# The ab times wo3 product of four token groups in Strassen's seven block products

## The chip, the cores and the metric

One core of one Trainium2 chip runs the whole kernel. The metric is the device time of one execution in microseconds (us), lower is better. TensorE does the matmuls, VectorE, ScalarE and GpSimd the work on tiles, and SyncE (SP) issues the DMAs.

## The reference

Attention with 32 packed rows per head gives x of 4608 tokens by 512 columns; a gated layer and a second layer follow. The part that the change touches is the second layer:

```python
x = np.ascontiguousarray(attn_out.transpose(0, 2, 1, 3)).reshape(B * S, H * D)
x = _moe_ref(x=x, **moe_kwargs)              # silu(x@w_gate) * (x@w_val) @ w_out, d_ff 1536
# _moe2_ref: d_model 512, d_ff 1024
a = x @ w1
b = x @ w2
h = a * b @ w3
return (h @ w_out).astype(np.float32)
```

## The kernel before

w3 @ w_out is made once, in float32, as `wo3` (1024 by 512) while the gated layer runs, and lies in the DRAM tile `wo3d`. The last part of the kernel then takes the 4608 tokens in six groups of 768, g = 0 to 5 in the code and 1 to 6 in the text. Each group has two stages.

*Stage 5* makes ab, a times b, transposed, in eight steps f (0 to 7) of 128 columns each. a and b come out of seven block products by Strassen's scheme (`PROD`: bank, sum of x blocks, sum of weight blocks). A product is six matmuls of 128x128 by 128x384 (L1012): each operand is split into a high and a low float32r part, and three of the four cross terms are taken. ScalarE copies four of the products out of PSUM (`keep`, L1027), VectorE and GpSimd add the others to them (`comb`, L1032) and multiply (L1059, L1060). `split` casts the high part on ScalarE (L96) and subtracts it for the low part (L89) on VectorE or GpSimd. The split of a step's ab into `abh` and `abl`, 128x768, is done in the next step, behind its second product.

*Stage 7* multiplies ab by wo3, which lies split in SBUF (`wo_hi`, `wo_lo`), for six tiles of 128 tokens: eight steps f by three terms of 128x128 by 128x512 (L1076). ScalarE copies each tile out (L1078), and SP stores it.

Around this, `x2_prep` loads the next group's x in three, then one DMA of 384 KB (`x2_load`, L831), makes sums of blocks on VectorE (L836) and splits seven of them. The weights' block sums `ws` are made in group 1, each stored to `wsd`, and loaded again in groups 2 to 6, one DMA of 256 KB a product, two steps ahead (`ahead`, L826); step 0's stay in SBUF. In the gated layer `w3_task` fits the work on w3 into free slots; `pin` keeps some of its conversions from being moved earlier by the scheduler.

The engines run their instructions in the order of the program here (`manual_schedule` for the engines in `M0`), and SP issues its DMAs in order too: a DMA that waits holds up those behind it.

Of the kernel before, what the change touches and what calls it, by code (L numbers as in the profile page):

```python
# [8 lines left out]
F32 = mybir.dt.float32  # L9
# [4 lines left out]
ALU = mybir.AluOpType  # L14
# [24 lines left out]
def packed_attention_moe_kernel(  # L39
# [777 lines left out]
    def ws_block(f, k):  # L817

        t = ws_tile(0, f, k)
        split(t[:, 0], t[:, 1], wsrc[f][PROD[k][1]], sub_on="pool" if k % 2 else "dve")  # L820
        if f:
            nc.sync.dma_start(wsd[f, k], t.bitcast(F32).rearrange("p h (d n) -> p h d n", d=2))

    def ws_load(g, f, k):
        t = ws_tile(g, f, k)
        nc.sync.dma_start(t.bitcast(F32).rearrange("p h (d n) -> p h d n", d=2), wsd[f, k])  # L826

    def x2_load(g, i, j):
        t = xp.tile([128, 2, TH], F32, tag="x2r", name=f"x2r{g}_{i}{j}", bufs=3)
# [169 lines left out]
    def split_wo3(r):  # L999
        split(wo3_hi[:, r], wo3_lo[:, r], wo3_t.pop(r))  # L1000

    def stage5(g, f):
        bk = {n: bank(f"p{n}{g}_{f}")[:, 0:TH] for n in "ABC"}
        A, Bk, Cb = (bk[n] for n in "ABC")

        def product(k, first):
            n, _, name = PROD[k]
            xh, xl = x2_t[g, name]
            w = ws_t[f, k]
            for d in range(2):  # L1010
# [128 lines left out]
```

## Time and profile before

| | |
|---|---|
| median of 3 runs | 1357.03 us (1355.51 to 1357.6) |
| profiled execution, its own time | 1358.21 us |
| its span in the profile | 1356.4 us |
| TensorE busy | 1333.3 us, 98% |
| VectorE, ScalarE, GpSimd busy | 48%, 42%, 28% |
| moved by DMA | 230.27 MB, 170 GB/s over the span |
| granted TensorE clock | full in every slice |

Busy time is the sum of what an engine's instructions last, overlaps counted once. A TensorE that is busy for 98% leaves little to wait for, but its matmuls overlap in the pipeline, so the time from the start of one to the start of the next tells more than its duration.

### The profile page before, as it was taken

To read this page: it belongs to the slowest core of one execution; us is meant where nothing else is said; L and a number is where in the kernel's file an instruction comes from. 1 tells how busy PE (TensorE), PEld (TensorE's weight loads), DVE (VectorE), ACT (ScalarE), POOL (GpSimd) and SP (SyncE) were. 2 spreads that over 40 slices of the span, in tenths; PEclk is the share of its full clock that TensorE was granted. 3 is DMA by queue.
4 is the path that set the end of the run, shared out by engine and by line. 5 is a ranking of instruction groups with operands and counts; after the bars stand their busy time and mean duration, and the time that the engine had idled before them with its cause. 6 is when DMAs were issued, how large, how long until landed. Compare 5 with 4: busy or idle time off the path is not lost.

```text
span 1356.4 us, 25516 instructions
## 1 busy us (share of the span) xinstructions
PE 1333.3 (98%) x10196; PEld 1237.9 (91%) x10196; DVE 655.0 (48%) x962; ACT 569.1 (42%) x940; POOL 386.4 (28%) x309
## 2 busy tenths in 40 slices
PE   7889999999999999999999999999999999999998
PEld 5679899999999999999999999899899899998997
DVE  4766877336564466453454389623323334234230
ACT  5774644344443444345544247433333333333331
POOL 1333322323322233244444236312012021121120
PEclk9999999999999999999999999999999999999999
DMA  9977766534545444244453259737458276284441
GB/s 307 345 237 213 220 194 188 167 86 116 153 132 182 122 112 125 71 163 122 129 162 109 74 179 340 277 104 254 147 155 254 81 220 208 94 253 158 143 145 47
DMA packets 186822, 230.27 MB, mean 170 GB/s; under 512 B 70736, under 2 KB 117840, under 8 KB 186704
## 3 DMA queue, kind: packets, MB, share of 16 engines
q1 hardware_dynamic: 186704, 228.64, 53.8%
q8 instruction: 81, 1.33, 0.4%
q14 instruction: 37, 0.30, 0.1%
HBM read 179.04 MB, written 49.55 MB: 169 GB/s over the span
## 4 chain that ended last, share of the span: by engine, by line
PE 81%; DVE 4%; DMA 1%; issue 1%; ACT 1%; SPq 0%; DVEq 0%; ACTq 0%
PE px L674 20%; PE po L1076 14%; PE pA L1012 13%; PE pg L445 10%; PE pv L445 9%; PE pB L1012 6%; PE pw L766 3%; PE pC L1012 3%; PE pc L412 2%; DVE ws L89 1%; PE psq L209 1%; DMA wo3r<-wo3d 0%; DMA x2r<-X2d 0%; DVE x2T L836 0%; DMA X2d<-acc 0%
## 5 line engine op out<-in xcount | busy, mean ns | idle before, releaser
L89 POOL TENSOR_TENSOR ul<-u,uh 128x576 fp32r<-128x576 f32 x96 | 145.7, 1519 | 303.4 <-ACT uh L96 281.5
L1032 POOL TENSOR_TENSOR c<-s,s 128x384 f32<-128x384 f32 x48 | 49.2, 1024 | 376.8 <-ACT s L1027 376.6
L674 PE MATMUL px<-uh,woh 128*128 128x384 f32 x576 | 147.7, 337 | 0.2
L674 PE MATMUL px<-ul,woh 128*128 128x384 f32 x576 | 146.3, 334 | 0.0
L674 PE MATMUL px<-uh,wol 128*128 128x384 f32 x576 | 146.3, 334 | 0.0
L1027 ACT COPY s<-pA 128x384 f32<-128x384 f32 x144 | 69.0, 479 | 179.8 <-PE pA L1012 172.0
L454 DVE TENSOR_TENSOR u<-u,pv 128x576 f32<-128x576 f32 x96 | 71.9, 749 | 134.9 <-PE pv L445 121.1
L1076 PE MATMUL po<-wo_hi,abh 128*128 128x512 f32 x288 | 112.2, 389 | 0.4 <-ACT abh L96 0.4
L1076 PE MATMUL po<-wo_hi,abl 128*128 128x512 f32 x288 | 112.3, 390 | 0.3 <-DVE abl L89 0.3
L1076 PE MATMUL po<-wo_lo,abh 128*128 128x512 f32 x288 | 112.2, 389 | 0.0
L686 DVE TENSOR_TENSOR acc<-acc,px 128x768 f32<-128x768 f32 x72 | 68.1, 950 | 85.1 <-PE px L674 84.6
L674 PEld LDWEIGHTS px<-uh,woh 128*128 128x128 f32 x576 | 102.5, 188 | 6.0 <-issue 3.3
L96 ACT CAST uh<-u 128x576 fp32r<-128x576 f32 x96 | 64.6, 674 | 103.1 <-DVE u L454 102.7
L674 PEld LDWEIGHTS px<-uh,wol 128*128 128x128 f32 x576 | 104.1, 188 | 0.0
L674 PEld LDWEIGHTS px<-ul,woh 128*128 128x128 f32 x576 | 104.0, 188 | 0.0
L450 ACT ACTIVATE u<-pg 128x576 f32<-128x576 f32 x96 | 62.4, 650 | 96.5 <-PE pg L445 90.7
L89 POOL TENSOR_TENSOR wol<-wof,woh 128x512 fp32r<-128x512 f32 x48 | 65.2, 1368 | 127.3 <-ACT woh L96 124.6
L89 DVE TENSOR_TENSOR abl<-ab,abh 128x768 fp32r<-128x768 f32 x48 | 48.1, 1002 | 105.1 <-ACT abh L96 105.0
L445 PE MATMUL pg<-aTh,ch 128*128 128x288 f32 x384 | 83.9, 300 | 1.2 <-DVE cl L89 0.8
L445 PE MATMUL pv<-aTh,ch 128*128 128x288 f32 x384 | 82.9, 297 | 0.9 <-DVE cl L89 0.6
L445 PE MATMUL pg<-aTh,cl 128*128 128x288 f32 x384 | 82.3, 296 | 0.5 <-DVE cl L89 0.5
L445 PE MATMUL pg<-aTl,ch 128*128 128x288 f32 x384 | 82.4, 296 | 0.0
(308 smaller groups left out, 3082.6 us busy)
## 6 DMA issues: line engine op xcount, KB each, us to landing
ws<-wsd SPq DMA_DIRECT2D x245, 256.0 KB, 3.0
wf<-Wd SPq DMA_DIRECT2D x36, 512.0 KB, 5.7
wsd<-ws SPq DMA_DIRECT2D x49, 256.0 KB, 3.2
km<-in_k_dram SPq DMA_DIRECT2D x16, 576.0 KB, 7.6
wof<-wod SPq DMA_DIRECT2D x36, 256.0 KB, 3.0
x2r<-X2d SPq DMA_DIRECT2D x24, 384.0 KB, 5.3
out_dram<-o SPq DMA_DIRECT2D x36, 256.0 KB, 2.0
vm<-in_v_dram SPq DMA_DIRECT2D x16, 512.0 KB, 8.9
```

The lines of the kernel that those rows point to most:

```text
L89: x = eng.tensor_tensor(out=out, in0=src, in1=hi.bitcast(F32), op=ALU.subtract)
L96: nc.scalar.copy(hi, src)
L445: nc.tensor.matmul(t[:, hf, 0:HS], lhsT=w[:, b % 2, Q, cols], rhs=x[:, Q, hf, :], start=first, stop=last,)
L450: x = nc.scalar.activation(u, t[:, :, 0:HS], AF.Silu)
L454: x = nc.vector.tensor_tensor(out=u, in0=u, in1=t[:, :, 0:HS], op=ALU.mult)
L674: nc.tensor.matmul(t[:, h, 0:CW], lhsT=w[:, 128 * d:128 * d + 128], rhs=x[:, CW * c:CW * c + CW], start=first, stop=last,)
L686: pin_at["acc"] = nc.vector.tensor_tensor(out=o, in0=o, in1=t[:, :, 0:CW], op=ALU.add)
L766: nc.tensor.matmul(t[:, 1], lhsT=a[:, kk], rhs=w, start=(i == 0), stop=(i == 11))
L1012: nc.tensor.matmul(bk[n], lhsT=w[:, hl, 128 * d:128 * d + 128], rhs=r[:, d], start=(first and d == 0 and i == 0), stop=(d == 1 and i == 2) ...
L1027: nc.scalar.copy(o, t)
L1032: on.tensor_tensor(out=r, in0=o, in1=t, op=op)
L1076: nc.tensor.matmul(t, lhsT=a[:, j, cols], rhs=w[:, f], start=first, stop=last)
```

## The change

From group 3 on (`GS` = 2 in the code's count) stage 7 becomes `stage7s`: ab in 2x2 blocks of tokens and columns, wo3 in 2x2 blocks, and seven products by the same `PROD`. Each is 3 tiles of tokens x 4 pairs of steps x 3 terms of 128x128 by 128x256. The products add up in PSUM banks A and B, three each, and in four SBUF tiles kA to kD. Stage 5 of these groups splits sums of ab's blocks (`pair_tasks`: A11, S1 to S4, A12, A22, each 128x384) one behind each product of the next step.

wo3's seven sums of blocks are made in group 2 (`wob_task`: four pairs i of rows, each with two loads, four subtracts, seven splits and seven stores to `wobd`), in eight half tiles of the weights' pool. They are loaded again for each product, 1 MB each, three products ahead; for group 3 the first three are loaded during its stage 5. The ws weights are laid out in pairs and, from group 3 on, loaded two products a time, 512 KB, into five buffers, step 0's too. x2's loads stand ahead of the new stage's loads of sums, and its other work behind the products 0, 1 and 2. In `w3_task` the pin no longer covers the conversions; by the scheduler's order four of them (w3_0_0 to w3_0_3, each an activation and a cast on ScalarE) then stand some steps earlier in the gated layer.

```diff
-    wsd = tc.dram_tile([NF2, 7, 128, 2, 2, 128], F32, name="wsd")
+    wsd = tc.dram_tile([NF2 * 7 // 2, 128, 2, 2, 256], F32, name="wsd")
+    wobd = tc.dram_tile([7, 128, NF2 // 2, 2, 256], F32, name="wobd")
...
+            if NH <= i < 2 * NH:
+                pin.update(dve=w3_at[1], act=w3_at[2])
             new = tuple(int(x) for x in w3_list[i - 1].split("_")[1:])
+            pin.clear()
...
-            if NH <= i < 2 * NH:
-                pin.update(dve=w3_at[1], act=w3_at[2])
             w3_conv(w3_list[i])
-            pin.clear()
...
+    GS = 2
+    NPB = NF2 // 2
+    pair_t, wob_t, abT, later = {}, {}, {}, []
+    def ws_pair(n):
+        if n >= (NG2 - GS) * 28:
+            return
+        at, tag = (wgv, ("wh", "wl")[n % 5 % 2]) if n % 5 < 4 else (mp2, "wsx")
+        t = at.tile([128, 2, 2, 256], F32R, tag=tag, name=f"wsp{n}")
+        nc.sync.dma_start(t.bitcast(F32).rearrange("p a h n -> p (a h n)"),
+                          wsd[n % 28].rearrange("p a h n -> p (a h n)"))
+        pair_t[n] = t
...
+    def wob_load(n):
+        if n >= (NG2 - GS) * 7:
+            return
+        if n % 3 == 0:
+            t = [vl.tile([128, 2, 256], F32R, tag=("vt", "vu")[i % 2], name=f"wob{n}_{i}") for i in range(NPB)]
+            for i in range(NPB):
+                nc.sync.dma_start(t[i].bitcast(F32), wobd[n % 7][:, i])
+        else:
+            x = mp2.tile([128, NPB, 2, 256], F32R, tag="wob", name=f"wob{n}", bufs=2)
+            nc.sync.dma_start(x.bitcast(F32).rearrange("p i h n -> p (i h n)"),
+                              wobd[n % 7].rearrange("p i h n -> p (i h n)"))
+            t = [x[:, i] for i in range(NPB)]
+        wob_t[n] = t
...
+    def wob_task(i, n):
+        if n == 0:
+            e, o = (vl.tile([128, DM], F32, tag="vt", name=f"wo3e{i}_{r}") for r in range(2))
+            for r, t in enumerate((e, o)):
+                nc.sync.dma_start(t, wo3d[1, 2 * i + r])
+            b = wo3_b[i] = {"B11": e[:, 0:256], "B12": e[:, 256:512], "B21": o[:, 0:256], "B22": o[:, 256:512]}
+            return
+        b = wo3_b[i]
+        if n == 1:
+            t = xp.tile([128, 4, 256], F32, tag="wf", name=f"wo3s{i}")
+            for at, (name, x, y) in enumerate((("T1", "B12", "B11"), ("T2", "B22", "T1"),
+                                               ("T3", "B22", "B12"), ("T4", "B21", "T2"))):
+                nc.vector.tensor_tensor(out=t[:, at], in0=b[x], in1=b[y], op=ALU.subtract)
+                b[name] = t[:, at]
+            return
+        k = n - 2
+        if (7 * i + k) % 2 == 0:
+            wo3_b["to"] = wgv.tile([128, 2, 2, 256], F32R, tag=("wh", "wl")[(7 * i + k) // 2 % 2], name=f"wobs{i}_{k}")
+        t = wo3_b["to"][:, (7 * i + k) % 2]
+        split(t[:, 0], t[:, 1], b[PROD[k][2]], sub_on="pool" if k % 2 else "dve")
+        nc.sync.dma_start(wobd[k][:, i], t.bitcast(F32))
...
+    wob_at = {}
+    for i in range(NPB):
+        wob_at[max(2 * i, 0), 3 if i else 5] = [(i, 0)]
+        for n in range(1, 7):
+            wob_at[2 * i + 1, n] = [(i, n)]
+        if i + 1 < NPB:
+            wob_at[2 * i + 2, 1], wob_at[2 * i + 2, 2] = [(i, 7)], [(i, 8)]
...
+    def block(i, name, src, on):
+        hl = tuple(mp2.tile([128, TH], F32R, tag=f"{name}{x}{i}", name=f"{name}{x}{i}") for x in "hl")
+        split(*hl, src, sub_on=on)
+        abT[i, name] = hl
+    def pair_tasks(f, ab0, ab1):
+        i = f // 2
+        tt = nc.vector.tensor_tensor
+        if f % 2 == 0:
+            def s3():
+                t = mp2.tile([128, TH], F32, tag="s3t", name=f"s3t{i}")
+                nc.gpsimd.tensor_tensor(out=t, in0=ab0[:, 0], in1=ab0[:, 1], op=ALU.subtract)
+                block(i, "S3", t, "pool")
+            return [lambda: block(i, "A11", ab0[:, 0], "dve"), s3]
+        def s1():
+            tt(out=ab0[:, 1], in0=ab0[:, 1], in1=ab1[:, 1], op=ALU.add)
+            block(i, "S1", ab0[:, 1], "dve")
+        def s2():
+            tt(out=ab0[:, 0], in0=ab0[:, 1], in1=ab0[:, 0], op=ALU.subtract)
+            block(i, "S2", ab0[:, 0], "dve")
+        def s4():
+            tt(out=ab1[:, 0], in0=ab1[:, 0], in1=ab0[:, 0], op=ALU.subtract)
+            block(i, "S4", ab1[:, 0], "dve")
+        return [s1, s2, lambda: block(i, "A12", ab1[:, 0], "pool"), s4, lambda: block(i, "A22", ab1[:, 1], "pool")]
...
-            if f and 0 < ng < NG2:
+            if f and 0 < ng < GS:
                 ws_load(ng, nf + 1, k)
+            if g == GS - 1 and f == 0:
+                ws_store(0, k)
+            i = 56 * (g - GS) + 7 * f + k
+            if g >= GS and i % 2:
+                pair_t.pop(i // 2)
+                ws_pair(i // 2 + 5)
+            if g == GS - 1:
+                for x in wob_at.pop((f, k), ()):
+                    wob_task(*x)
+            if g >= GS and 0 < k < 6 and later:
+                later.pop(0)()
...
+            tag, h = {"s1": (0, 0), "c11": (0, 0), "s5": (0, 1), "c22": (0, 1),
+                      "s2": (1, 0), "c12": (1, 0), "s3": (1, 1)}[name]
+            tag = ("kA", "kB", "kC", "kD")[2 * (f % 2) + tag]
+            if tag not in half:
+                half[tag] = mp2.tile([128, 2, TH], F32, tag=tag, name=f"{tag}{g}_{f}")
+            return half[tag][:, h]
...
+            ab_t[f % 2] = ab
+            later.extend(pair_tasks(f, ab_t[0], ab))
+            return
...
+    def stage7s(g):
+        bkA, bkB = ([bank(f"po{n}{g}_{m}")[:, 0:256] for m in range(3)] for n in "AB")
+        bk = {"A": bkA, "B": bkB, "C": bkB}
+        kt = {n: mp2.tile([128, 3, 256], F32, tag=n, name=f"{n}{g}") for n in ("kA", "kB", "kC", "kD")}
+        def put(j, h, o, ms=slice(0, 3)):
+            r0 = 2 * TH * g + TH * j
+            nc.sync.dma_start(
+                out[r0 + 128 * ms.start:r0 + 128 * ms.stop, 256 * h:256 * h + 256].rearrange("(m p) n -> p m n", p=128),
+                o[:, ms])
+        for k, (n, a, _) in enumerate(PROD):
+            first = k in (0, 1, 5)
+            w = wob_t.pop(7 * (g - GS) + k)
+            for m in range(3):
+                for i in range(NPB):
+                    ah, al = (x[:, 128 * m:128 * m + 128] for x in abT[i, a])
+                    for q, (l, h) in enumerate(((ah, 0), (ah, 1), (al, 0))):
+                        nc.tensor.matmul(bk[n][m], lhsT=l, rhs=w[i][:, h],
+                                         start=(first and i == 0 and q == 0), stop=(i == NPB - 1 and q == 2),
+                                         skip_group_check=not first)
+                if m == 2:
+                    wob_load(7 * (g - GS) + k + 3)
+                t = bk[n][m]
+                if k in (0, 1, 2, 6):
+                    o = kt[("kA", "kB", "kC", None, None, None, "kD")[k]]
+                    if k == 6 and m == 2:
+                        nc.vector.tensor_copy(o[:, m], t)
+                    else:
+                        nc.scalar.copy(o[:, m], t)
+                    if k == 6:
+                        put(1, 0, o, slice(m, m + 1))
+                else:
+                    o = kt[{3: "kC", 4: "kB", 5: "kA"}[k]]
+                    nc.vector.tensor_tensor(out=o[:, m], in0=o[:, m], in1=t, op=ALU.add)
+            if k in (3, 4, 5):
+                put(*{3: (0, 1), 4: (1, 1), 5: (0, 0)}[k], o)
+            if g + 1 < NG2 and k < 3:
+                x2_prep(g + 1, k + 1)
...
+                if g == GS and f in (2, 4, 6):
+                    wob_load(f // 2 - 1)
+            if g < GS:
+                ab_split.pop()()
+                if g == GS - 1:
+                    wob_task(NPB - 1, 7)
+                    wob_task(NPB - 1, 8)
                 for part in range(4):
                     x2_prep(g + 1, part)
-            stage7(g)
-    mp.release()
-    wst.release()
+                if g == GS - 1:
+                    for n in range(4):
+                        ws_pair(n)
+                stage7(g)
+            else:
+                if g + 1 < NG2:
+                    x2_prep(g + 1, 0)
+                while later:
+                    later.pop(0)()
+                stage7s(g)
+            if g == GS - 1:
+                assert not wob_at
+                mp.release()
+                wst.release()
+                mp2 = pool("mp2", "right")
+                ws_pair(4)
+    mp2.release()
```

On TensorE, this is where stage 7 of group 3 begins: before, the first tile of tokens (`po_0`) over the steps' `abh` and `abl`.

```order
L1076 MATMUL po_0_11997<-wo_hi,abh_0_11389 128x512
L1076 MATMUL po_0_11997<-wo_lo,abh_0_11389 128x512
L1076 MATMUL po_0_11997<-wo_hi,abl_0_11390 128x512
L1076 MATMUL po_0_11997<-wo_hi,abh_1_11469 128x512
L1076 MATMUL po_0_11997<-wo_lo,abh_1_11469 128x512
L1076 MATMUL po_0_11997<-wo_hi,abl_1_11470 128x512
```

With the change, product 0 (`poA_0` to `poA_2` are its tiles of tokens, `wob_0` to `wob_3` the pairs of wo3's sum, high and low part):

```order
L1225 MATMUL poA_0_12118<-wob_0_11680,A11h_11539 128x256 x2
L1225 MATMUL poA_0_12118<-wob_0_11680,A11l_11540 128x256
L1225 MATMUL poA_0_12118<-wob_1_11681,A11h_11708 128x256 x2
L1225 MATMUL poA_0_12118<-wob_1_11681,A11l_11709 128x256
L1225 MATMUL poA_0_12118<-wob_2_11682,A11h_11871 128x256 x2
L1225 MATMUL poA_0_12118<-wob_2_11682,A11l_11872 128x256
L1225 MATMUL poA_0_12118<-wob_3_11683,A11h_12034 128x256 x2
L1225 MATMUL poA_0_12118<-wob_3_11683,A11l_12035 128x256
L1225 MATMUL poA_1_12119<-wob_0_11680,A11h_11539 128x256 x2
```

A matmul now has 256 columns where it had 512, there are more of them, and x2 marks two rows that read alike (by the sum's high and its low part).

On ScalarE, this is step 5 of group 2: before, four copies out of PSUM and the split of the step before.

```order
L1027 COPY s_1_5_10882<-pA_5_10873 128x384
L1027 COPY s_1_5_10892<-pB_5_10874 128x384
L96 CAST abh_4_10871<-ab_4_10868 128x768
L1027 COPY s_1_5_10904<-pA_5_10873 128x384
L1027 COPY s_1_5_10924<-pA_5_10873 128x384
```

With the change, casts of wo3's sums (`wobs`, from the loaded rows `wo3e` and their sums `wo3s`) stand between the copies:

```order
L1147 COPY s_1_5_10961<-pA_5_10952 128x384
L1147 COPY s_1_5_10971<-pB_5_10953 128x384
L96 CAST abh_4_10950<-ab_4_10947 128x768
L1147 COPY s_1_5_10988<-pA_5_10952 128x384
L96 CAST wobs_0_10992<-wo3e_0_10913 128x256
L96 CAST wobs_0_10992<-wo3s_10977 128x256
L1147 COPY s_1_5_11015<-pA_5_10952 128x384
L96 CAST wobs_2_11021<-wo3s_10977 128x256
L96 CAST wobs_2_11021<-wo3e_1_10914 128x256
L96 CAST wobs_4_11046<-wo3s_10977 128x256
```

Two casts now stand behind the third copy and ahead of the fourth, the first from a tile that a DMA issued in step 4 loads, the second from a difference that VectorE makes of it.

On SP, this is stage 7 of group 3: before, four loads of x and six stores of out.

```order
L831 DMA x2r_00_11953<-X2d 128x2x384
L831 DMA x2r_01_11955<-X2d 128x2x384
L831 DMA x2r_11_11957<-X2d 128x2x384
L831 DMA x2r_10_11965<-X2d 128x2x384
L1080 DMA out_dram<-o_0_12022 128x512
L1080 DMA out_dram<-o_1_12050 128x512
L1080 DMA out_dram<-o_2_12078 128x512
L1080 DMA out_dram<-o_3_12106 128x512
L1080 DMA out_dram<-o_4_12134 128x512
L1080 DMA out_dram<-o_5_12162 128x512
```

With the change, from x2's last load on, the loads of sums (`wob`, for the products 4 to 6 of this group, then 0 and 1 of the next) and the stores of kC, kB, kA and kD:

```order
L838 DMA x2r_10_12181<-X2d 128x2x384
L1031 DMA wob_12227<-wobd 128x2048
L1031 DMA wob_12278<-wobd 128x2048
L1028 DMA wob_0_12333<-wobd 128x512
L1028 DMA wob_1_12334<-wobd 128x512
L1028 DMA wob_2_12335<-wobd 128x512
L1028 DMA wob_3_12336<-wobd 128x512
L1214 DMA out_dram<-kC_12126 128x3x256
L1031 DMA wob_12381<-wobd 128x2048
L1214 DMA out_dram<-kB_12125 128x3x256
L1031 DMA wob_12423<-wobd 128x2048
L1214 DMA out_dram<-kA_12124 128x3x256
```

Each store now stands behind the load of a sum, kA's behind that for product 1 of the next group.

## Rows read from the trace of the kernel before

**Rows 1.** the page: engine TensorE, and the chain that ended last by line.
```profile
PE 1333.3 (98%) x10196; PEld 1237.9 (91%) x10196; DVE 655.0 (48%) x962; ACT 569.1 (42%) x940; POOL 386.4 (28%) x309
...
PE px L674 20%; PE po L1076 14%; PE pA L1012 13%; PE pg L445 10%; PE pv L445 9%; PE pB L1012 6%; PE pw L766 3%; PE pC L1012 3%; PE pc L412 2%; DVE ws L89 1%; PE psq L209 1%; DMA wo3r<-wo3d 0%; DMA x2r<-X2d 0%; DVE x2T L836 0%; DMA X2d<-acc 0%
```

**Rows 2.** table of windows cut at stages 5 and 7, columns in its head.
```profile
core 0: us, PE busy (x) PEld busy (x) DVE busy (x) ACT busy (x) POOL busy (x), PEclk, DMA share, GB/s
802.60:863.91 61.31, 60.12 (x337) 57.90 (x337) 54.18 (x95) 38.65 (x95) 38.20 (x37) 1.00 0.91 326
...
897.89:956.13 58.24, 58.24 (x337) 58.24 (x336) 18.82 (x30) 20.34 (x40) 15.31 (x16) 1.00 0.68 215
956.13:988.82 32.69, 32.69 (x146) 27.03 (x146) 11.34 (x13) 9.11 (x13) 0.90 (x1) 1.00 0.32 109
```

**Rows 3.** the longest piece of the chain in group 3's stage 7.
```profile
1047.22 32.68 PE po L1076 x144
```

**Rows 4.** TensorE's timeline: start, duration, then line and operation.
```profile
396.10 0.42 PE L445 MATMUL pg<-aTl,ch 128*128 128x288 f32 x2
...
403.57 0.42 PE L445 MATMUL pg<-aTh,cl 128*128 128x288 f32 x2
...
62.76 1.09 PE L510 MATMUL pk<-ident,km 128*128 128x128 f32 x8
...
L510 PE MATMUL pk<-ident,km x128: 272/273/477, 5.3 to 74.7; 128*128 128x128 f32 x128
```

**Rows 5.** two weight loads behind a stall in group 1's stage 7, timeline.
```profile
869.32 0.19 PEld L1076 LDWEIGHTS po<-wo_hi,abh 128*128 128x128 f32 x1 [0.87 <-ACT abh L96]
...
869.43 0.19 PEld L1076 LDWEIGHTS po<-wo_lo,abh 128*128 128x128 f32 x1
```

**Rows 6.** one of ScalarE's copies in group 2's stage 5, timeline.
```profile
899.13 0.48 ACT L1027 COPY s<-pA 128x384 f32<-128x384 f32 x1 [0.41 <-PE pA L1012]
```

**Rows 7.** group 1's stage 5, a late copy, timeline.
```profile
815.30 0.48 ACT L1027 COPY s<-pA 128x384 f32<-128x384 f32 x1
...
815.67 0.41 ACT L96 CAST ws<-wsa 128x256 fp32r<-128x256 f32 x1
815.84 0.19 PEld L1012 LDWEIGHTS pA<-xT3h,ws 128*128 128x128 f32 x1 [0.43 <-ACT s L1027]
...
815.98 0.42 ACT L96 CAST ws<-wsb 128x256 fp32r<-128x256 f32 x1
```

**Rows 8.** groups of instructions in group 1's stage 5, by form.
```profile
L1027 ACT COPY s<-pA 128x384 f32<-128x384 f32 x24 | 11.5, 480 | 21.1 <-PE pA L1012 13.3 <-DMA X2d<-acc 6.6 <-DVE ws L89 1.2
...
L1032 POOL TENSOR_TENSOR c<-s,s 128x384 f32<-128x384 f32 x8 | 8.8, 1095 | 5.0 <-ACT s L1027 4.9
...
L89 DVE TENSOR_TENSOR ws<-wsa,ws 128x256 fp32r<-128x256 f32 x7 | 6.2, 880 | 1.5 <-ACT ws L96 1.5
...
L1032 DVE TENSOR_TENSOR c<-s,pB 128x384 f32<-128x384 f32 x8 | 4.3, 542 | 0.0
...
L801 DVE TENSOR_TENSOR wsa<-wsa,w12r 128x256 f32<-128x256 f32 x7 | 3.0, 424 | 0.2
```

**Rows 9.** windows with the highest DMA rates, and the page's DMA issues.
```profile
50.00:75.00 25.00, 20.78 (x435) 14.92 (x434) 19.27 (x48) 19.57 (x38) 8.11 (x6) 1.00 1.08 345
825.00:850.00 25.00, 25.00 (x143) 24.16 (x142) 24.90 (x44) 17.53 (x44) 18.80 (x19) 1.00 0.95 341
...
ws<-wsd SPq DMA_DIRECT2D x245, 256.0 KB, 3.0
...
out_dram<-o SPq DMA_DIRECT2D x36, 256.0 KB, 2.0
```

**Rows 10.** x2's work in group 3's stage 7, by form.
```profile
L836 DVE TENSOR_TENSOR x2T<-x2r,x2T 128x768 f32<-128x768 f32 x2 | 1.9, 954 | 1.6 <-DMA x2r<-X2d 1.6
```

**Rows 11.** ScalarE ahead of the w3 conversions, timeline.
```profile
591.68 0.65 ACT L450 ACTIVATE u<-pg 128x576 f32<-128x576 f32 x1 [7.99 <-PE pg L445]
```

**Rows 12.** the end of the kernel, timeline.
```profile
1352.76 0.58 ACT L1078 COPY o<-po 128x512 f32<-128x512 f32 x1 [4.85 <-PE po L1076]
```

More of the change, by code (lines that the diff above doesn't have):

```diff
@@ L821, in ws_block, with ws_at, ws_store @@
         if f:
-            nc.sync.dma_start(wsd[f, k], t.bitcast(F32).rearrange("p h (d n) -> p h d n", d=2))
+            ws_store(f, k)
+    def ws_at(f, k):
+        i, half = divmod(7 * f + k, 2)
+        return wsd[i][:, half]
+    def ws_store(f, k):
+        nc.sync.dma_start(ws_at(f, k), ws_t[f, k].bitcast(F32))
     def ws_load(g, f, k):
-        t = ws_tile(g, f, k)
-        nc.sync.dma_start(t.bitcast(F32).rearrange("p h (d n) -> p h d n", d=2), wsd[f, k])
+        nc.sync.dma_start(ws_tile(g, f, k).bitcast(F32), ws_at(f, k))
     def x2_load(g, i, j):
@@ new lines, in packed_attention_moe_kernel @@
+    wo3_b = {}
+    def wob_task(i, n):
[19 more added lines that the diff above has]
+        nc.sync.dma_start(wobd[k][:, i], t.bitcast(F32))
@@ L1004, in stage5 @@
         A, Bk, Cb = (bk[n] for n in "ABC")
+        mpx = mp if g < GS else mp2
+        half = {}
         def product(k, first):
@@ L1008, in product @@
             xh, xl = x2_t[g, name]
-            w = ws_t[f, k]
+            i = 56 * (g - GS) + 7 * f + k
+            w = ws_t[f, k] if g < GS else pair_t[i // 2][:, i % 2]
             for d in range(2):
@@ L1021, in ahead, with at @@
             ng, nf = divmod(n, NF2 - 1)
-            if f and 0 < ng < NG2:
+            if f and 0 < ng < GS:
                 ws_load(ng, nf + 1, k)
+            if g == GS - 1 and f == 0:
+                ws_store(0, k)
+            i = 56 * (g - GS) + 7 * f + k
+            if g >= GS and i % 2:
[6 more added lines that the diff above has]
+                later.pop(0)()
+        def at(name):
+            if g < GS:
+                return mp.tile([128, TH], F32, tag=name, name=f"{name}_{g}_{f}")
+            tag, h = {"s1": (0, 0), "c11": (0, 0), "s5": (0, 1), "c22": (0, 1),
[4 more added lines that the diff above has]
+            return half[tag][:, h]
         def keep(name, t):
-            o = mp.tile([128, TH], F32, tag=name, name=f"{name}_{g}_{f}")
+            o = at(name)
             nc.scalar.copy(o, t)
@@ L1030, in comb @@
         def comb(name, t, o, op=ALU.add, on=nc.vector):
-            r = mp.tile([128, TH], F32, tag=name, name=f"{name}_{g}_{f}")
+            r = at(name)
             on.tensor_tensor(out=r, in0=o, in1=t, op=op)
@@ L1057, in stage5 @@
         ahead(6)
-        ab = mp.tile([128, 2, TH], F32, tag="ab", name=f"ab{g}_{f}")
+        assert not later
+        ab = mpx.tile([128, 2, TH], F32, tag=f"ab{f % 2 if g >= GS else ''}", name=f"ab{g}_{f}")
         nc.gpsimd.tensor_tensor(out=ab[:, 1], in0=c12, in1=c22, op=ALU.mult)
         nc.vector.tensor_tensor(out=ab[:, 0], in0=c11, in1=A, op=ALU.mult)
+        if g >= GS:
+            ab_t[f % 2] = ab
+            later.extend(pair_tasks(f, ab_t[0], ab))
+            return
         abh = mp.tile([128, 2, TH], F32R, tag="abh", name=f"abh{g}_{f}", bufs=NF2)
@@ L1094, in packed_attention_moe_kernel @@
                         load_wo3(f + 1)
-            ab_split.pop()()
-            if g + 1 < NG2:
+                if g == GS and f in (2, 4, 6):
+                    wob_load(f // 2 - 1)
+            if g < GS:
+                ab_split.pop()()
+                if g == GS - 1:
+                    wob_task(NPB - 1, 7)
+                    wob_task(NPB - 1, 8)
                 for part in range(4):
                     x2_prep(g + 1, part)
-            stage7(g)
-    mp.release()
-    wst.release()
+                if g == GS - 1:
[15 more added lines that the diff above has]
+    mp2.release()
     wgv.release()
```

## The prediction

> **What bounds the kernel now.** I read the page first, then the table of windows, then the timelines. On the page the reader is to see TensorE busy for 98% of the span, and a chain of waits that runs through its matmuls almost alone, L1076 and L1012 of this last part among them [rows 1]. The windows cut that part at the starts of stage 5 and stage 7 [rows 2]. Only group 1 has holes. From 897.89 on TensorE has none: 58.24 us for 336 matmuls of 384 columns and 32.69 us for 144 of 512, while VectorE, ScalarE and GpSimd are busy for at most 20.34 of the 58.24 us and DMA moves 215 GB/s. The clock stands at 1.00, the 2.4 GHz level, in every window, so I change nothing for it. So time is won here only by a shorter list of matmuls, and lost only where another engine or a DMA makes TensorE wait, which it does not do now.
>
> **The saving.** Stage 7 of groups 3 to 6 goes from 144 matmuls of 512 columns to 7 x 3 x 4 x 3 = 252 of 256. Columns fall by 1 - 252 x 256 / (144 x 512) = 12.5%, but what counts is the time from one matmul to the next. 512 columns: 32.68 / 144 = 226.9 ns [rows 3]. 384: 58.24 / 336 = 173.3 [rows 2]. 288: from 396.10 to 403.57 lie 28 rows of two, 7.47 / 56 = 133.4 [rows 4]. The three lie on a line, 0.416 to 0.419 ns a column and 13.4 ns besides. At 256 it gives 120.1 ns. Nothing in the trace alternates a full 128x128 load with 256 columns, so I bound it. From above: it takes no longer than 288 columns, 133.4. From below: eight pairs of load and 128-column matmul take 1.09 us, of which the last matmul is 0.27, so 0.82 / 7 = 117 ns a pair [rows 4]. There the weight load sets the pace, for 128 columns are fewer than 256. The load that follows a stall comes 0.10 to 0.11 us behind the first [rows 5], which still fits under 120. I take the line, being nearest to the 288 row: 252 x 120.1 = 30.27 us, **2.42 us saved a group, 9.7 in four**. The bounds are 4 x (32.69 - 29.48) = 12.8 saved and 4 x (33.62 - 32.69) = 3.7 lost; the break-even is 32.69 / 252 = 129.7 ns.
>
> The Trainium skill's "TensorE: Matmul & The Clock Gate", section "Back-to-back issue gap", gives N/2.4 + 2.5 ns for an isolated matmul, and says that with a weight load before each one both set the spacing. By its formula the saving would be 144 x 215.8 - 252 x 109.2 ns = 3.6 us a group, 14.2 in all; our row for 512 columns, 226.9, is 11 ns above it, so the rows decide.
>
> **What the cut block products add in groups 3 to 6.** Where a copy or a split is late, TensorE stops for the lateness and about 0.1 us more for a new load [rows 5]. How narrow it is in stage 5: ScalarE's copy starts 0.24 us after its product ends (899.13 against 897.89 + 1.04), takes 0.48, and its bank is wanted one product (1.04 us) later, or 0.17 sooner for the load: 0.15 to 0.3 us of slack [rows 6]. Now up to five splits of 384 columns come between, each one cast on ScalarE and one subtract of 0.55 on VectorE or 1.0 to 1.1 on GpSimd [rows 8]. ScalarE starts its next instruction 0.37 us after a copy of 384 columns and 0.31 after a cast of 256 [rows 7]. ScalarE then has 2.3 + 5 x 0.4 us of 7.28 a step, GpSimd 2.0 + 2 to 3. Placed behind each product they fit. I take 0.3 us in all; the upper bound is the slack's size at each of some 12 places, 3.6.
>
> **Group 2 (wo3's sums).** Steps 1 to 7 gain four T subtracts and seven splits for each of four blocks. Group 1 shows what the like does: a cast ahead of a copy, and TensorE's load behind the copy that begins at 815.30 is 0.43 us late [rows 7]. In three even steps a cast stands between abh and the copy s2: the cast's 0.31 minus the slack is 0.24, and up to 0.45 more where GpSimd and VectorE subtract at once (880 ns by 424 [rows 8]). **1.0 us**, bounds 0 and 1.5.
>
> The larger cost there is the queue. From step 1 to 5 SP issues 7 loads of ws, and 5 stores in an odd step or 2 stores and 2 loads of wo3 in an even one: 12, 11, 12, 11, 12 transfers of 0.262 MB, 15.2 MB in 36.4 us, 417 GB/s. The trace's most over 25 us is 345, and 341 at a share of 0.95, so 359 at a full one [rows 9]. So a backlog grows: at 345 a step drains 2.51 MB, and when the two loads for block i=2 are issued, after product 3 of step 4, 0.63 + 0.37 + 0.63 + 0.21 = 1.84 MB lie ahead (5.3 us), besides some 2 us that SP lost in step 1 by waiting, in order, for the first splits' stores. Issued at 33.3 from the stage's start, with a lead of 1.7 (256 KB land in 2.0 to 3.0 us on a free queue [rows 9], of which 0.8 is their own moving) and that 0.8, they land at about 43.5. Wanted: ScalarE casts from them behind s2 of step 5, and s3 stands behind those casts; s3 must start by 36.4 + 5.6 = 42.0 us, with a subtract (0.42) and two casts in between, so the load must land by 41.1. Late by 2.7 us at 345, 1.5 at 359, 0.3 at 375, 4.0 at 330. TensorE then stops for it, the queue drains, and block i=3 costs little more. **2.0 us**, bounds 0.3 and 7 (7 at 300 GB/s, near group 1's 326 [rows 2]). The ws loads themselves lead by two steps, 14.6 us, and come in time. The Trainium skill's "DMA: Bandwidth & Descriptors", section "Specifications", has about 358 GB/s of HBM for one core; by that alone the term would be 1.5.
>
> **Loads in stage 7.** A group's new stage moves 7 x 1.05 MB of sums, 1.57 of x2, 1.57 of out and 0.52 of ws: 11 MB in 30.3 us, 364 GB/s, where 110 flowed before [rows 2]. Each sum is issued two products (8.6 us) before it is wanted and takes 3 us of a full queue; x2's last block, issued behind VectorE's split of B11 at about 8.5, lands near 11.5. VectorE's x2 work, 4 + 7 tensor ops at 0.95 [rows 10], then ends at 18, and its three sums for k=3 at 19, wanted at 21.6. These fit. What doesn't quite is the store of kA: it is queued behind a 1 MB load issued at 25.9 and lands at 31.5 to 32.8, while ScalarE's first copy of the next group, into the same buffer, is wanted at 31.5. 0 to 1.3 us in each of three groups: **1.5**. In stage 5 the ws pairs ask 14.7 MB in 58.24 us, 252 GB/s (305 in group 3 with three sums), below the rates above: nothing.
>
> **The rest.** Four conversions of w3 move in ScalarE's and VectorE's order to where ScalarE idles 7.99 us before 591.68 [rows 11], some 20 us earlier; TensorE waits for none now: 0, give or take 1. At the end a copy of 0.58 and a store of 256 KB follow the last matmul [rows 12]; half the size makes it 0.3 less.
>
> **Sum.** -9.7 + 0.3 + 1.0 + 2.0 + 1.5 - 0.3 = -5.2 us. The profiled execution took 1358.2 (span 1356.4), so 1353.0; against the median of 1357.0, **1351.8**.
>
> **Rivals.**
> - *Slower: the pair is bound by its weight load at 256 columns.* If it takes 133 ns like 288 columns, stage 7 takes 33.6, and with 4.5 of costs the kernel takes 1357.0 + 3.7 + 4.5 = 1365. It is slower from 32.69 - 4.5/4 = 31.57, 125.3 ns. For it: a load's row lasts 0.19 us [rows 5]. Against: loads follow at 0.10 and pairs at 117 ns. 0.07.
> - *The queue in group 2 keeps only 300 to 320 GB/s*, since loads and stores are mixed at 2 KB. Then 5 to 7 us are lost there: 1355 to 1357, and with the kA stores at their worst 1359. Against: 341 was reached with the same mix. 0.15.
> - *Copies late in every even step of groups 3 to 6*, as in group 1: 12 x 0.3 + 12 x 0.1: 4.8, so 1356.3. For it: the slack is so small. 0.12.
> - *More is won:* no wait costs anything, or the interval is 117 ns: 1357.0 - 9.7 - 0.3 + 0.5 = 1347.5 down to 1344.5. 0.10. By the formula of the Trainium skill's section on the issue gap, named above, with the same costs of 4.5, the time would be 1357.0 - 14.2 + 4.5 = 1347.3, in this case's stretch; the 226.9 of the trace speaks against it.
>
> **How the numbers follow.** The forecast as it stands, 1349 to 1354, has 0.56. 0.2% is 2.7 us, about what a measurement can tell from no change: same is 1354.3 to 1359.7. Faster: 0.56 + 0.10 and a little of the second and third, 0.68. Same: the rest of those two, 0.18. Slower: the first and the tails, 0.14. The range 1346.5 to 1360 leaves out the first rival and the lowest of the last.
>
> **What would show it.** L1225's matmuls should start every 120 ns (129.7 or more kills the saving). The stages 7 of groups 3 to 6 should last 30.3 us, with no idle before them. Group 2's stage 5 should be 61 us, with TensorE waiting for ScalarE's copy in steps 5 and 7, and ScalarE for the load wo3e. At the start of groups 4 to 6 the first copy should wait for the store of kA. I am wrong if TensorE stands still inside the new stage 7, or in stage 5 of groups 3 to 6.

## The result: slower by 1.3%

The changed kernel takes 1375.36 us in the median of 4 runs (1369.93 to 1377.94), the kernel before 1356.87 (1355.51 to 1357.6). The ratio is 1.0132, with a 95% interval of 1.0101 to 1.0164. The profiled execution took 1375.24 us, its span is 1373.5.

TensorE is as busy as before [rows 1], 1333.1 us by 1333.3, in a longer span. The page of the kernel after:

```profile
PE 1333.1 (97%) x10628; PEld 1255.8 (91%) x10628; DVE 736.6 (54%) x1114; ACT 608.4 (44%) x1068; POOL 466.0 (34%) x385
```

The table of windows of the kernel after, cut where stages 5 and 7 begin as in [rows 2] (stage 5 of group 2, then of group 3, its new stage 7, and so on; the last row is group 6's new stage 7 with the end):

```profile
901.47:969.33 67.86, 61.31 (x337) 59.37 (x336) 36.20 (x57) 29.18 (x66) 25.46 (x25) 0.97 0.83 279
...
1002.01:1060.68 58.67, 58.67 (x338) 58.15 (x337) 27.33 (x45) 26.37 (x56) 29.85 (x30) 1.00 0.86 295
1060.68:1090.67 29.99, 29.99 (x254) 29.99 (x253) 17.12 (x27) 11.10 (x23) 2.81 (x3) 1.00 0.92 323
1090.67:1151.73 61.06, 58.51 (x338) 58.19 (x337) 27.14 (x46) 25.42 (x55) 29.58 (x29) 1.00 0.81 264
1151.73:1181.75 30.02, 30.02 (x253) 30.02 (x253) 17.09 (x27) 11.01 (x23) 3.91 (x4) 1.00 0.89 301
1181.75:1247.67 65.92, 61.97 (x338) 61.66 (x337) 26.97 (x46) 25.69 (x55) 29.87 (x30) 0.95 0.76 247
...
1277.71:1340.16 62.45, 59.84 (x339) 59.52 (x338) 27.14 (x46) 25.42 (x55) 29.56 (x29) 0.97 0.69 236
1340.16:1373.50 33.34, 30.15 (x253) 29.94 (x252) 8.03 (x17) 5.97 (x16) 3.08 (x4) 1.00 0.53 174
```

The last row's counterpart before:

```profile
1319.84:1356.40 36.56, 32.84 (x145) 26.84 (x144) 1.51 (x2) 4.36 (x7) 0.90 (x1) 1.00 0.12 43
```

Read the first number behind the window and the clock (third from the end). The new stage 7 lasts 29.99 to 30.04 us where it lasted 32.69; the end with group 6's stage 33.34 for 36.56. But stage 5, 58.24 in each of groups 2 to 6 before, is 67.86 in group 2, 61.06, 65.92 and 62.45 in groups 4 to 6, and the clock is below 1.00 in three of these four. Group 1 begins at 806.51 instead of 802.60. By places, in us of the span: 3.9 before group 1, -0.3 in group 1, 9.6 in group 2, 0.4 in group 3's stage 5, 14.7 in the stages 5 of groups 4 to 6, and -11.2 in the four new stages and the end. That is 17.1, the whole difference of the spans.

The table of waits of the kernel after, TensorE's three longest in the part from 560 us on (who waited for whom, us in total, times, the longest):

```profile
PE pA L1111 <- ACT kA L1147: 9.1, 3, 3.9
PE pA L1111 <- ACT s L1147: 7.2, 5, 2.8
PE pc L413 <- DVE acc L687: 3.0, 1, 3.0
```

None of them was there before, but for a part of the second, which lies in group 1. They name the three places: kA at the start of groups 4 to 6, the copies s in group 2 (with group 1's own), and acc in the gated layer.

### The profile page after: what moved, and what is told of

Same layout as the page of the kernel before. It is cut to its first block, busy times and chain, and to the rows that moved or that the text cites. A ratio compares the mean times of both kernels' runs of the same rounds, so it can differ in the third digit from the quotient of the medians.

```text
span 1373.5 us, 26602 instructions
## 1 busy us (share of the span) xinstructions
PE 1333.1 (97%) x10628; PEld 1255.8 (91%) x10628; DVE 736.6 (54%) x1114; ACT 608.4 (44%) x1068; POOL 466.0 (34%) x385
## 4 chain that ended last, share of the span: by engine, by line
PE 80%; DMA 5%; DVE 3%; issue 1%; ACT 1%; SPq 0%; POOL 0%; ACTq 0%; DVEq 0%
PE px L675 19%; PE pA L1111 14%; PE pg L446 9%; PE pv L446 9%; PE pB L1111 7%; PE po L1201 4%; PE poA L1225 4%; PE poB L1225 4%; PE pC L1111 3%; PE pw L767 3%; PE pc L413 2%; DMA out_dram<-kA 2%; DMA ws<-wsd 1%; PE psq L210 1%; DMA wo3r<-wo3d 0%
## 5 line engine op out<-in xcount | busy, mean ns | idle before, releaser
L446 PE MATMUL pv<-aTh,cl 128*128 128x288 f32 x384 | 82.1, 295 | 0.0
L446 PE MATMUL pv<-aTl,ch 128*128 128x288 f32 x384 | 82.1, 295 | 0.0
L446 PEld LDWEIGHTS pg<-aTh,ch 128*128 128x128 f32 x384 | 63.0, 188 | 9.3 <-DVE u L455 3.2
L89 DVE TENSOR_TENSOR cl<-pc,ch 128x1024 fp32r<-128x1024 f32 x48 | 56.8, 1217 | 26.4 <-ACT ch L425 26.4
L446 PEld LDWEIGHTS pv<-aTh,ch 128*128 128x128 f32 x384 | 61.7, 188 | 2.0 <-DVE cl L89 0.8
L446 PEld LDWEIGHTS pg<-aTh,cl 128*128 128x128 f32 x384 | 61.9, 189 | 0.7 <-DVE cl L89 0.7
```

Of the source, the lines that this page charges most:

```text
L89: x = eng.tensor_tensor(out=out, in0=src, in1=hi.bitcast(F32), op=ALU.subtract)
L446: nc.tensor.matmul(t[:, hf, 0:HS], lhsT=w[:, b % 2, Q, cols], rhs=x[:, Q, hf, :], start=first, stop=last,)
```

## Experiments

**The buffer that waits for its store.** The chain of waits of the kernel after, at the start of group 5 (start, duration, what):

```profile
1169.06 4.32 PE poA L1225 x36
1173.38 4.23 PE poB L1225 x36
...
1179.37 7.95 DMA out_dram<-kA
...
1187.42 0.49 ACT kA L1147
...
1187.95 2.29 PE pA L1111 x6
```

The store of kA is issued at 1179.37 and lands 7.95 us later; only then does ScalarE make the first copy of the next group into kA, 5.7 us after that group began at 1181.75. Two edits try this. One gives step 0 the buffers kC and kB, so that kA is written a step later:

```diff
-            tag = ("kA", "kB", "kC", "kD")[2 * (f % 2) + tag]
+            tag = ("kC", "kB", "kA", "kD")[2 * (f % 2) + tag]
```

> Step 0 of each group writes its copies to kC and kB, and kA and kD are used from step 1 on. My theory: TensorE's waits of 2.5 to 3.9 us at the start of groups 4 to 6, and the half clock behind two of them, hang on the store of kA alone; the three stages 5 fall from 61.1, 65.9 and 62.5 us to 58.3 to 58.8, and the time from 1375 to about 1361 (1359 to 1363). Rival: the DMA queue is full at that place whatever the buffer; then the copies or the products wait for the next store or for the pairs of ws, and the time stays above 1370.

Measured: 1360.7 us (ratio to before 1.0033, 1.0023 to 1.0043), 14.7 less than the change. Its windows of groups 4 to 6:

```profile
1089.12:1147.36 58.24, 58.24 (x338) 58.24 (x337) 27.15 (x46) 25.55 (x55) 29.57 (x29) 1.00 0.85 278
1177.39:1235.64 58.25, 58.25 (x339) 58.25 (x338) 27.15 (x46) 25.55 (x55) 29.59 (x29) 1.00 0.83 278
1265.66:1323.91 58.25, 58.25 (x338) 58.25 (x337) 27.15 (x46) 25.55 (x55) 29.59 (x29) 1.00 0.76 253
```

All three stages 5 are back at 58.24 or 58.25 and the clock at 1.00, with the same loads and stores in the queue. So it was the buffer; the wait did not go to another DMA, and the rival falls. The store itself is no faster here: it still takes 7.2 us in the median, but nothing waits for it.

The other edit leaves the buffer, and issues the store ahead of the load that stands before it:

```diff
-                if m == 2:
+                if m == 2 and k != 5:
                     wob_load(7 * (g - GS) + k + 3)
...
                 put(*{3: (0, 1), 4: (1, 1), 5: (0, 0)}[k], o)
+            if k == 5:
+                wob_load(7 * (g - GS) + k + 3)
```

> The store of kA is issued ahead of the load of the sum that is issued behind product 5, so that no load that is ready at the same time stands ahead of it in the queue. My theory, as in the prediction: the load ahead is what makes it late; it lands 3 to 5 us after its issue, TensorE's waits at the start of groups 4 to 6 fall to under 1 us, and the time to about 1362. Rival: what is issued behind the store shares the engines with it; it still takes 7 to 8 us, is issued at most 1.3 us earlier, and the time falls by 2 to 5 us only, to 1370 to 1373.

Measured: 1363.27 us (1.0051, 1.0034 to 1.0068), 12.1 us of the 14.7. The stores of kA, us from issue to landing (least, median, most), of the kernel after and of this one:

```profile
DMA to landing us min/median/max: 2.6/7.8/8.0
```

```profile
DMA to landing us min/median/max: 2.6/5.4/6.2
```

The 2.6 is the store of the last group, with nothing in the queue ahead of it. What stood ahead of the others is in SP's order, here for the store at the end of group 4, of the kernel after and of this one:

```profile
1173.64 0.42 SPq L1031 DMA_DIRECT2D wob<-wobd  x1
1174.14 0.55 SPq L1214 DMA_DIRECT2D out_dram<-kB  x1
1176.58 2.70 SPq L1028 DMA_DIRECT2D wob<-wobd  x4
1179.37 0.44 SPq L1214 DMA_DIRECT2D out_dram<-kA  x1
```

```profile
1170.10 0.42 SPq L1031 DMA_DIRECT2D wob<-wobd  x1
1170.59 0.53 SPq L1214 DMA_DIRECT2D out_dram<-kB  x1
1174.67 0.39 SPq L1214 DMA_DIRECT2D out_dram<-kA  x1
```

In the kernel after, the first load (1 MB) lands 9.1 us after its issue, at 1182.7, kB's store 9.6 after, at 1183.7, the four loads (1 MB together) at 1184.3 to 1186.3, and kA's store behind them at 1187.3. So none of the six had landed when it was issued: 2.5 MB. In this kernel the four loads stand behind it, but the first load (8.8 us) and kB's store (9.3) are still in flight, 1.4 MB, until 1179.9; kA's store lands at 1180.9. The other groups are alike: 7.7 to 8.0 us with 2.2 to 2.5 MB ahead, 5.0 to 6.2 with 1.2 to 1.4 MB. The theory, 3 to 5 us to landing and about 1362, was right that the load ahead makes the store late, but left out the load before that one and kB's store. The rival's reason, what is issued behind, is not needed for these times and not shown.

TensorE's waits for kA fall from 9.1 to 1.5 us in all. The three stages 5 still take 59.07, 60.46 and 59.33 us, 4.1 above 58.24; most of the 2.6 beside the waits are matmuls that start 177 ns apart instead of 173 through most of groups 5 and 6, at a clock of 1.00, and why is open.

**The moved conversions.** VectorE's timeline of the kernel after, ahead of TensorE's wait:

```profile
590.70 0.71 DVE L750 STREAM_TRANSPOSE w3T(0, 1)_7561<-vt_w 128x512 f32<-128x512 f32 x1 [1.45 <-POOL w3l(0, 0)_7495 L89]
591.33 0.92 DVE L687 TENSOR_TENSOR acc<-acc,px 128x768 f32<-128x768 f32 x1
...
593.24 1.53 DVE L354 SCALAR_TENSOR_TENSOR vt_w<-vt_w,vx_w 128x512 int32<-128x512 int32 x1 [0.66 <-ACT vt_w L350]
594.88 0.71 DVE L750 STREAM_TRANSPOSE w3T(0, 2)_7656<-vt_w 128x512 f32<-128x512 f32 x1
595.51 0.92 DVE L687 TENSOR_TENSOR acc<-acc,px 128x768 f32<-128x768 f32 x1
```

The transpose at 590.70 waited for GpSimd's w3l, and the sums acc, which TensorE's banks hang on, stand behind that and other work of w3, the third of them at 595.51. Before the change such sums came each as soon as its matmuls were done:

```profile
586.91 0.95 DVE L686 TENSOR_TENSOR acc<-acc,px 128x768 f32<-128x768 f32 x1 [2.17 <-PE px L674]
590.03 0.95 DVE L686 TENSOR_TENSOR acc<-acc,px 128x768 f32<-128x768 f32 x1 [2.17 <-PE px L674]
```

TensorE's timeline of the kernel after shows what this cost:

```profile
592.43 1.09 PE L413 MATMUL pc<-wf,PTd 64*32 64x256 f32 x32
596.48 3.34 PE L413 MATMUL pc<-wf,PTd 64*32 64x256 f32 x64 [2.95 <-DVE acc L687]
```

32 matmuls take 1.09 us ahead of the wait and 64 take 3.34 behind it, some 1.2 more than at the same pace: the granted clock is 0.51 from 596.48 to 599.40. So the wait of 2.95 and the clock make some 4.1, for the 3.9 found by places. The edit puts the pin around the conversions as it was:

```diff
-            if NH <= i < 2 * NH:
-                pin.update(dve=w3_at[1], act=w3_at[2])
             new = tuple(int(x) for x in w3_list[i - 1].split("_")[1:])
-            pin.clear()
...
+            if NH <= i < 2 * NH:
+                pin.update(dve=w3_at[1], act=w3_at[2])
             w3_conv(w3_list[i])
+            pin.clear()
```

> The pin covers the conversions of w3 as before the change, all else as after. My theory: TensorE's wait of 3.0 us for acc at 593 us comes from VectorE's order there (a transpose of w3 that waits for GpSimd's w3l stands ahead of acc); stage 5 of group 1 begins at 802.6 again instead of 806.5, and the time is 1371 to 1372. Rival: the 3.9 us come from another place, as the other ws layout or DMA, and stay: 1375.

Measured: 1370.05 us (1.0104, 1.0089 to 1.012). VectorE's timeline there, and the window of group 1's stage 5:

```profile
587.16 0.95 DVE L687 TENSOR_TENSOR acc<-acc,px 128x768 f32<-128x768 f32 x1 [2.17 <-PE px L675]
590.28 0.95 DVE L687 TENSOR_TENSOR acc<-acc,px 128x768 f32<-128x768 f32 x1 [2.17 <-PE px L675]
```

```profile
802.86:863.86 61.00, 60.13 (x337) 57.89 (x337) 54.12 (x95) 38.66 (x95) 38.31 (x37) 1.00 0.94 329
```

The sums come every 3.12 us again, TensorE's wait of 3.0 us for acc is gone, and group 1 begins at 802.86. The cost was the moved work, not the layout of ws. Of the 5.3 us that the median falls, more than the 3 to 4 expected, 3.7 lie before group 1 in the profile; where the rest lies is not shown.

**Group 2: the rows that are loaded again.** Without their loads, with the high part in SBUF in their place (so the sums leave out the low part):

```diff
-            e, o = (vl.tile([128, DM], F32, tag="vt", name=f"wo3e{i}_{r}") for r in range(2))
-            for r, t in enumerate((e, o)):
-                nc.sync.dma_start(t, wo3d[1, 2 * i + r])
+            e, o = (wo3_hi[:, 2 * i + r].bitcast(F32) for r in range(2))
```

> In group 2 the rows of wo3 are read from the high part that lies in SBUF instead of being loaded again, so the low part is left out of the sums; 8 of 78 transfers go, every cast, subtract and store stays. My theory: ScalarE's casts wait for these late loads; without them group 2's stage 5 falls from 67.9 to 59 to 62 us, and the time to 1367 to 1369. Rival: the casts and subtracts themselves make the copies late; then stage 5 stays above 65 and the time at 1373 to 1375. Second rival: the waits go to another DMA, the stores of the sums or the loads of ws; then ScalarE or TensorE waits for these, 1370 to 1374.

Measured: 1370.09 us (1.0099, 1.0082 to 1.0117). The window of group 2's stage 5:

```profile
901.16:961.06 59.90, 59.40 (x338) 58.00 (x337) 35.26 (x57) 28.95 (x66) 25.80 (x25) 1.00 0.79 281
```

59.90 us with all casts and subtracts in place, so these cost at most 1.7 us together and the loads the other 8. The median falls by 5.3 only and misses the 1367 to 1369 expected. But its runs spread from 1366.14 to 1372.05 (mean clock 0.996 in the first, 0.993 in the last), and the profiled one is the fastest: its span, 1364.4, is 9.1 under that of the kernel after. The stages 5 of groups 4 to 6 still have the wait for kA's store, so the window of group 2 tells more here than the median.

Why the loads were so late is in ScalarE's timeline and SP's waits of the kernel after, group 2:

```profile
927.30 0.48 ACT L1147 COPY s<-pA 128x384 f32<-128x384 f32 x1
931.30 0.41 ACT L96 CAST wobs<-wo3e 128x256 fp32r<-128x256 f32 x1 [3.52 <-DMA wo3e<-wo3d]
...
950.75 0.40 ACT L96 CAST wobs<-wo3e 128x256 fp32r<-128x256 f32 x1 [4.00 <-DMA ws<-wsd]
```

```profile
SPq L1059 <- DVE wobs L89: 11.8, 4, 4.1
```

ScalarE's cast from wo3e waits 3.52 us at 931.30 in step 3 and 4.00 in step 5, and the copies s behind it come late. (At 950.75 the view names ws, but wo3e's own load lands at 950.7, just ahead of the cast.) TensorE then waits for the copies, the first time 2.34 us until 932.60; the window behind that:

```profile
932.60:938.00 5.40, 5.40 (x22) 5.29 (x23) 5.18 (x8) 1.85 (x5) 3.54 (x4) 0.68 0.74 224
```

Two more such waits, of 2.77 and 1.28 us, end at 952.00 and 956.67. The clock has a part in the 9.6 us too: 0.68 over the 5.4 us behind the first wait is 1.7 us lost. SP waits 11.8 us for splits, whose stores stand in its order ahead of loads. All kernels from here on have the two mends above together, kA's buffer and the pin; first these by themselves:

> The two mends together: step 0's copies in kC and kB, and the pin over the conversions as before. If the two costs are separate, they add: 14.7 and 4 off 1375, so 1356 to 1357, no difference from before. Rival: mending the one only moves the wait to the other's place or into group 2; then 1359 or more.

Measured: 1358.01 us (1.0008, 0.9999 to 1.0017): no difference from before that this measurement tells, and 1 us above the 1356 to 1357 expected. The sum of the two gains, 14.7 and 5.3, would have given 1355.4; its trace has 1.4 us of TensorE's waits for the load of a sum in the new stage 7, which the kernel after does not have. Then the stores of the sums are put three products later:

```diff
-        nc.sync.dma_start(wobd[k][:, i], t.bitcast(F32))
+        wob_out.append((wob_out_at[0], wobd[k][:, i], t))
+
+    def wob_stores(now):
+        while wob_out and wob_out[0][0] + 3 <= now:
+            _, at, t = wob_out.pop(0)
+            nc.sync.dma_start(at, t.bitcast(F32))
...
             if g == GS - 1:
+                wob_out_at[0] = 7 * f + k
+                wob_stores(7 * f + k)
...
+                    wob_stores(99)
```

> As the two mends, and each store of wo3's sums is issued three products later, when its split is long done, so that SP does not wait for it in order. First theory for group 2: SP's waits for the splits (11.8 us, one of 4.1) keep the loads behind them from being issued, and the queue could have moved more than 293 GB/s; then stage 5 of group 2 falls from 67.7 to 60 to 63 us and the time to 1350 to 1353. Second theory: the queue itself moves no more than 295 GB/s of this mix; then SP's waits are only a sign of it, stage 5 stays above 65 and the time at 1355 to 1357.

Measured: 1352.26 us (0.997, 0.9958 to 0.9982). The window of group 2's stage 5 with the two mends alone, and with the late stores:

```profile
896.60:964.62 68.02, 61.59 (x338) 59.59 (x337) 35.78 (x56) 29.32 (x66) 25.44 (x26) 0.97 0.81 279
```

```profile
899.17:960.50 61.33, 59.76 (x338) 58.37 (x336) 35.80 (x57) 29.13 (x66) 25.74 (x25) 1.00 0.88 309
```

Two windows inside it, 10.5 us from 4.5 us after its start on and the 16.5 us behind, of the kernel after and of this one:

```profile
906.00:916.50 10.50, 10.50 (x62) 10.50 (x61) 5.70 (x10) 4.66 (x11) 4.38 (x5) 1.00 0.72 223
916.50:933.00 16.50, 14.00 (x79) 13.22 (x78) 8.20 (x14) 6.95 (x16) 5.71 (x6) 1.00 0.95 330
```

```profile
903.70:914.20 10.50, 10.50 (x62) 10.50 (x62) 5.70 (x10) 4.67 (x11) 4.38 (x5) 1.00 0.86 272
914.20:930.70 16.50, 16.33 (x93) 15.90 (x92) 11.29 (x20) 7.43 (x17) 8.60 (x9) 1.00 1.00 346
```

The same work has 272 GB/s in place of 223 in the first window, since six loads of ws are issued there instead of three, and 346 behind. The second block's rows are issued 20.7 us after the group's start (24.1 in the kernel after), and ScalarE's waits for wo3e shrink to one of 1.0 us. So the queue could move more; SP's order kept it from that. The second theory falls.

**All three costs gone.** The two mends and the rows from SBUF:

> As the two mends, and the rows of wo3 read from the high part in SBUF (the low part is left out of the sums). If the three costs add, group 2's stage 5 takes 59.5 to 60.5 us, all later stages 58.3 and 30.0, and the time is 1347 to 1350, 0.5 to 0.7% under before. Rival: with one wait gone TensorE waits at the next, for ws or wob in groups 3 to 6: above 1352.

Measured: 1349.64 us (0.9953, 0.9939 to 0.9967), group 2's stage 5 at 59.86: as expected. The last kernel, with the two mends, keeps the whole sums. GpSimd makes the rows from wo3's two parts, only the four T sums are split, and the plain blocks are stored once from SBUF in group 1:

```diff
+    TK = (1, 2, 4, 6)
+    def wob_rows():
+        for k, r, c in ((0, 0, 0), (3, 1, 256), (5, 1, 0)):
+            for h, t in enumerate((wo3_hi, wo3_lo)):
+                src = t.bitcast(F32).rearrange("p (i r) n -> p i r n", r=2)[:, :, r, c:c + 256]
+                nc.sync.dma_start(wobd[k][:, :, h], src)
...
-                nc.sync.dma_start(t, wo3d[1, 2 * i + r])
+                nc.gpsimd.tensor_tensor(out=t, in0=wo3_hi[:, 2 * i + r].bitcast(F32),
+                                        in1=wo3_lo[:, 2 * i + r].bitcast(F32), op=ALU.add)
...
         k = n - 2
+        if k not in TK:
+            return
...
+                if g == 0:
+                    wob_rows()
                 stage7(g)
```

> As the two mends, and in group 2 only the four T sums are split: GpSimd adds wo3's high and low part again to get its rows, without a load, and the three plain blocks are stored straight from the split wo3 during stage 7 of group 1. Group 2's transfers go from 78 to 58 (261 GB/s), ScalarE's casts from 28 to 16. My theory: stage 5 of group 2 takes 58.3 to 59.3 us and the time is 1345 to 1348. Rival: GpSimd's adds of 1.4 us ahead of its comb make ab late and with it the copies, or the stores in group 1 delay x2: 1349 to 1353.

Measured: 1346.84 us (0.9937, 0.9924 to 0.9949), as expected, and faster than the kernel before. Its windows of group 2's and group 3's stage 5, and of group 3's new stage 7:

```profile
897.32:956.04 58.72, 58.52 (x338) 58.19 (x336) 31.92 (x55) 25.48 (x55) 29.85 (x27) 1.00 0.73 248
988.72:1046.97 58.25, 58.25 (x338) 58.24 (x337) 26.72 (x45) 26.13 (x56) 29.59 (x29) 1.00 0.87 298
1046.97:1076.96 29.99, 29.99 (x254) 29.99 (x254) 16.89 (x27) 11.12 (x23) 3.07 (x4) 1.00 0.91 313
```

Group 2 costs 0.5 us more than before the change, the stages 5 behind it nothing, and the four new stages give their 11 us whole.

## Why the prediction was wrong

Forecast were 1351.8 us in a range up to 1360; it was 1375.4.

- **The saving was right.** 29.99 us for 252 matmuls are 119.0 ns each, where the line gave 120.1; 2.7 us a group, and 11.2 in four with the end, for 9.7 and 0.3. The rival of the weight load falls.
- **The store of kA: the place was right, the size wrong by ten: 14.7 us for 1.5.** The step that failed is "it is queued behind a 1 MB load issued at 25.9 and lands at 31.5 to 32.8". First in, first out was right; what I left out is the rest of the queue. When the store was issued, the load before that one, or part of it, and kB's store had not landed either: 2.2 to 2.5 MB ahead for the 1 MB counted. In group 4 it was issued 27.6 us after its stage began and landed at 35.6. I also left out the clock. The wait of 3.95 us at the start of group 5 cost 7.7: 2.7 more for the granted clock behind it (0.67 over 8.05 us), and about 1.0 because its products then take 1.06 us instead of 1.04 to the stage's end, at a clock of 1.00. The cause of that last part is open.
- **Group 2: 9.6 us for 3.0.** The mechanism was the predicted one, ScalarE's cast from wo3e and the copy behind it, but in steps 3 and 5, not 5 and 7. The step that failed is "some 2 us that SP lost in step 1 by waiting". SP waited four times, 11.8 us in all, and the first time 4.1 us at once: the queue ran at 223 GB/s for 10.5 us, when it had time to get ahead. So the rows were late in step 3 already. The rival with 300 GB/s in group 2 came nearest (279 in the stage's mean), but by SP's order and not, as it said, by the mix of transfers. The clock behind the first wait added 1.7. The 1.0 us for copies behind casts was somewhat low: the kernel without the loads has 1.7 in all, above its bound of 1.5.
- **The moved conversions: 3.9 us for 0.** The step that failed is "TensorE waits for none now: 0". The place moved to had idle time on ScalarE, which I looked at, but acc on VectorE waited there behind a transpose that itself waits for GpSimd, and the clock fell behind that wait too.
- **The splits in groups 3 to 6 and the end were right:** 0.4 us in group 3's stage 5 for the 0.3 taken in all, none in groups 4 to 6 once kA's wait is gone, and 0.5 at the end for 0.3.
- **Two slips in its sums do not bear on this.** ScalarE's copy starts 0.20 us behind its product (899.13 by 898.93), not 0.24. The terms given for the rows of block 2 add up to 43.1 and not 43.5, which is 2.0 us late and not 2.7 at 345 GB/s; 2.0 is the term that was taken.

So three costs of 28 us in all stood against a gain of 11. All three are waits in the order of an engine or of SP. Another buffer and the pin take the first and the last away; later stores take most of group 2's (61.33 us for 68.02), which makes the change worth 0.3%, and rows made from SBUF nearly all of it, which makes it worth 0.6%.

## What to carry to other kernels

A tile that is stored at a stage's end should not be the first one written in the next stage: take a tile whose store is older, which cost nothing here. To tell when a store will land, count everything issued ahead of it that has not landed yet, and not the last transfer alone. In an engine's order or SP's, whatever waits for a slow chain (a store for its split, a sum for a transpose) should stand behind what others wait for, or be put a few steps later. And where TensorE is the bound without a hole, price a wait of a few us at up to twice its length (2.61 us cost 4.2, 3.95 cost 7.7), for the clock may fall behind it.

## What the hardware showed that was not expected

The clock behind a wait. Two windows of the kernel after, the 8 us behind the wait of 3.95 us at the start of group 5, and what follows:

```profile
1187.95:1196.00 8.05, 8.05 (x32) 8.05 (x33) 1.17 (x3) 1.29 (x3) 1.55 (x2) 0.67 0.49 171
1196.00:1200.00 4.00, 4.00 (x25) 4.00 (x24) 1.05 (x2) 2.21 (x5) 1.50 (x2) 1.00 0.75 249
```

The granted clock is 0.67 in the mean, and TensorE's timeline has matmuls of 384 columns 0.32 us apart at first, where they were 0.173 apart: the 1.2 GHz level instead of 2.4. The same level shows behind the waits of 2.34 us in group 2, 2.61 at the start of group 6 and 2.95 for acc, but not behind those of 2.55 (group 4) and 2.77 (group 2). In the kernel with kA's buffer alone, the same wait for acc, 2.96 us, has a clock of 1.00 behind it. So the length alone does not tell, and what does is left open. It also means that the price of a wait differs from run to run.

A store of 384 KB took 2.6 us with nothing ahead of it in the queue, 5.0 to 6.2 with 1.2 to 1.4 MB ahead that had not landed, and 7.7 to 8.0 with 2.2 to 2.5 MB. From 897 us on, none of SP's 278 DMAs before, 295 after and 295 in the kernel with the store first landed ahead of one that was issued earlier.
